# Softmax of seven units: exponential head by head out of the scores' bank

## The chip, the cores and the metric

One core of one Trainium2 chip. The metric is the device time of one execution in microseconds; the kernel before takes 1047.18 us as the median of three runs (1046.12 to 1047.91).

## The reference

Attention over pooled keys and values, then two gated feed-forward blocks. Cut to what matters:

```
k_p, v_p = k, v averaged over groups of 8 positions        # 72 pooled positions per head
scores   = (q @ k_p^T) / 8                                 # 4 batches, 8 heads, 576 queries
scores   = scores - max(scores, axis=-1)
attn     = exp(scores);  attn /= sum(attn, axis=-1) + 1e-9
x        = attn @ v_p, heads side by side                  # 2304 tokens x 512
x        = (silu(xn @ w_gate) * (xn @ w_val)) @ w_out      # xn: x normalised, d_ff = 1536
out      = ((x @ w_a) * (x @ w_b)) @ w_out2
```

## The kernel before

The 2304 tokens are cut in two ways. Attention works in nine units of 256 tokens (u = 0 to 8), each of two halves of 128 tokens (i = 0, 1). The first feed-forward block works on five tiles of 512, 256, 512, 512 and 512 tokens; per tile it goes through twelve hidden blocks f of 128: a gate product g, a value product v (12 matmuls each, every operand split in a high and a low part, hence wh and wl, xh and xl), a Silu of g on ScalarE, its product with v on VectorE (ht), the split of that product (hh on ScalarE, hl on VectorE), and the output product (acc, 12 matmuls). A bank each belongs to g, v and the four parts of acc; two banks (tag `att`) are shared by everything that attention puts into PSUM: transposed queries (qT), scores (sc), transposed exponentials (eT), the result (xT) and small sums.

Softmax of a unit, in `score_steps`: the queries are transposed and copied to SBUF (`q_transpose`), then `scores` makes two banks for each half, sc_0 and sc_1, with four heads of 72 columns in each. VectorE takes the maximum of each head (L328) and writes scores minus maximum into the SBUF tile e (L329). For units 2 to 8 `exponent` then runs one Exp over e of both halves (L335, 128 x 1152, in place), and `normalise` sums e per head (L340), adds 1e-9 (L341), takes reciprocals (L342) and multiplies (L343). Units 0 and 1 do this half by half. `value_steps` transposes e (eT) and multiplies it by the pooled values.

Attention of later units runs beside the feed-forward tiles. In tile 0 the order in which steps are emitted is a written list of tokens (FIRST), in tile 1 a second list, afterwards merged lists. The scheduler of the framework then sets each engine's queue: it places instructions by readiness and priority, so what stands in a queue can differ from the order in the source. Every engine works its own queue strictly in that order. Weights arrive as 64-bit words that ScalarE, VectorE and GpSimd turn into fp32 together (L590, L591 on ScalarE; L597, L600 on VectorE; L607 on GpSimd), and are split by ScalarE (L621) and GpSimd or VectorE (L622). The second feed-forward block (lines from L1015 on) starts at about 615 us and has no attention beside it.

ScalarE's functions live in tables; an ACT_TABLE_LOAD stands in its queue wherever the next function is not in the loaded one. Exp and Silu never share one here, while copies, casts, Square and Abs run under either.

Of the kernel before, what the change touches and what calls it, by code (L numbers as in the profile page):

```python
# [8 lines left out]
F32 = mybir.dt.float32  # L9
# [4 lines left out]
AF = mybir.ActivationFunctionType  # L14
ALU = mybir.AluOpType
AX = mybir.AxisListType

P = 128
# [4 lines left out]
FINE = 2  # L23
# [41 lines left out]
def attention_moe_moe2(  # L65
# [14 lines left out]
    nc = tc.nc  # L80
    B, H, S, D = q.shape
# [11 lines left out]
    QK_SCALE = 1.0 / float(D) ** 0.5  # L93
# [15 lines left out]
    sm_p = attn.enter_context(tc.tile_pool(name="sm", bufs=1, side="right"))  # L109
# [3 lines left out]
    for t0, n in starts(TILES1):  # L113
# [9 lines left out]
        out=mask, in_=mask, pattern=[[P, NV], [-SP, H]], compare_op=ALU.is_ge,  # L123
# [3 lines left out]
        out=mask, in_=mask, pattern=[[-P, NV], [SP, H]], compare_op=ALU.is_ge,  # L127
# [15 lines left out]
    def att_bank(name, tag=None):  # L143
        if tag is not None:
            pass
        else:
            tag = boot["banks"].pop(0) if boot["banks"] else "att"
        return ps.tile([P, 512], F32, tag=tag, name=name, bufs=2 if tag == "att" else 1)
# [118 lines left out]
    def runs(t0, n):  # L267
        done = 0
        while done < n:
            b, s = divmod(t0 + done, S)  # L270
            step = min(n - done, S - s)
            yield done, step, b, s
            done += step

    NU = NT // UNIT
    NS = UNIT // P
    q_t, e_t, xf_t = {}, {}, {}

    def load_q(sub):
        if sub >= NT // P:  # L280
            return
        t = at_p.tile([P, H, D], F32, tag="q", name=f"q_{sub}")
        for off, cnt, b, s in runs(sub * P, P):
            nc.sync.dma_start(
                out=t[off:off + cnt], in_=q[b, :, s:s + cnt, :].rearrange("h p d -> p h d")
            )
        q_t[sub] = t

    def score_steps(u):
        box = {}  # L290

        def q_transpose(i):
            sub = u * NS + i
            if i == 0:
                e_t[u] = at_p.tile([P, NS, H, SP], F32, tag="e", name=f"e_{u}")
            bank = att_bank(f"qT_{sub}")
            qs = q_t.pop(sub)
            for p in range(NP):
                nc.tensor.transpose(
                    bank[:, p * P:(p + 1) * P],  # L300
                    qs[:, 2 * p:2 * p + 2, :].rearrange("p a d -> p (a d)"),
                    ident,
                )
            if boot["on"] and i % 2:
                qT = h_p.tile([P, NP, P], F32, tag="ht", name=f"qTs_{sub}", bufs=1)
            else:
                qT = at_p.tile([P, NP, P], F32, tag="qT", name=f"qTs_{sub}", bufs=1)
            nc.scalar.copy(qT.rearrange("p a t -> p (a t)"), bank)
            box["qT"] = qT
            box["m"] = sm_p.tile([P, H, 1], F32, tag="m", name=f"m_{sub}", bufs=2)  # L310
            load_q(sub + NS)

        def scores(i, hf):
            sub, e, m, qT = u * NS + i, e_t[u], box["m"], box["qT"]
            sc = att_bank(f"sc_{sub}_{hf}")
            for off, cnt, b, s in runs(sub * P, P):
                for a in range(2):
                    p = 2 * hf + a
                    nc.tensor.matmul(  # L319
                        sc[off:off + cnt, a * 2 * SP:(a + 1) * 2 * SP],  # L320
                        qT[:, p, off:off + cnt],
                        KB[b % 2][:, p, :],
                        start=True,
                        stop=True,
                    )
            scv = sc[:, :4 * SP].rearrange("p (h s) -> p h s", h=4)
            mh = m[:, 4 * hf:4 * hf + 4, :]
            nc.vector.reduce_max(out=mh.rearrange("p h o -> p (h o)"), in_=scv, axis=AX.X)  # L328
            nc.vector.tensor_sub(  # L329
                e[:, i, 4 * hf:4 * hf + 4, :], scv, mh.to_broadcast([P, 4, SP])  # L330
            )

        def exponent(lo, hi):
            e = e_t[u][:, lo:hi].rearrange("p i h s -> p (i h s)")
            nc.scalar.activation(out=e, in_=e, func=AF.Exp, scale=QK_SCALE)  # L335

        def normalise(lo, hi):
            ev = e_t[u][:, lo:hi].rearrange("p i h s -> p (i h) s")
            sums = sm_p.tile([P, NS * H, 1], F32, tag="sums", name=f"sum_{u}")[:, :(hi - lo) * H]
            nc.vector.reduce_sum(out=sums.rearrange("p h o -> p (h o)"), in_=ev, axis=AX.X)  # L340
            nc.vector.tensor_scalar_add(sums, sums, 1e-9)  # L341
            nc.vector.reciprocal(sums, sums)  # L342
            (nc.gpsimd if boot["alt"] else nc.vector).tensor_mul(  # L343
                ev, ev, sums.to_broadcast([P, (hi - lo) * H, SP])
            )

        steps = []
        for i in range(NS):
            steps += [lambda i=i: q_transpose(i)]
            if u < FINE:  # L350
                steps += [lambda i=i, h=h: scores(i, h) for h in range(2)]
                steps += [lambda i=i: exponent(i, i + 1), lambda i=i: normalise(i, i + 1)]
            else:
                steps += [lambda i=i: (scores(i, 0), scores(i, 1))]
        if u >= FINE:
            steps += [lambda: exponent(0, NS), lambda: normalise(0, NS)]
        return steps

    def value_steps(u, dest):
# [312 lines left out]
    def dest(u):  # L672
        t = u * UNIT
        for idx, (t0, n) in enumerate(starts(TILES1)):
            if t0 <= t < t0 + n:
# [4 lines left out]
                return get  # L680

    A = [score_steps(u) for u in range(NU)]
    V = [value_steps(u, dest(u)) for u in range(NU)]
    loads, prep = zip(*(prep_steps(b) for b in range(B)))
# [497 lines left out]
    for idx, (ph, t0, n) in enumerate(work):  # L1182
# [26 lines left out]
        for f, cols, last, ahead, own in jobs:  # L1209
            m = cols.stop - cols.start  # L1210
# [31 lines left out]
        for c, acc in enumerate(accs):  # L1242
            ev = ev_p.tile([P, 512], F32, tag="ev", name="ev")
# [45 lines left out]
```

## Time and profile before

| | |
|---|---|
| median of three runs | 1047.18 us |
| the profiled execution, its own time | 1046.91 us |
| its span | 1045.0 us |
| mean granted TensorE clock | 0.98 of full speed |
| busy: TensorE, weight loads | 978.8 us (94%), 858.4 us (82%) |
| busy: VectorE, ScalarE, GpSimd | 663.0 us (63%), 477.0 us (46%), 453.0 us (43%) |

The profiled execution's own time is its span and 1.9 us around it. The shares are means over stages with different limits: the first 300 us have attention, weight conversion and the first tile beside each other, the stretch from 300 to 600 us is nearly all feed-forward matmuls. PE is TensorE, PEld its weight loads, DVE VectorE, ACT ScalarE, POOL GpSimd.

### The profile page before, as it was taken

Reading aid. Unit: us, or ns where it says so; the run is one execution under the profiler, and the core shown is the slowest. Engines: PE = TensorE matmul, PEld = TensorE weight load, DVE = VectorE, ACT = ScalarE, POOL = GpSimd, SP = SyncE. Lnnn points to the kernel's source line nnn. Section 1 sums busy time; section 2 is a strip of 40 time slices with the busy share of each in tenths; the row PEclk is TensorE's granted clock in tenths of the full one; section 3 lists DMA queues with packets and bytes.
Section 4 is the critical chain, followed back from the end, with each engine's and each line's share of the span. In section 5 each row is a group of like instructions: output and inputs, shape, how many; then the busy total and the mean of one; then the engine's idle time right before and its main releaser. Section 6 shows DMA issues by size and latency. Waiting matters only on the chain.

```text
span 1045.0 us, 13959 instructions
## 1 busy us (share of the span) xinstructions
PE 978.8 (94%) x5044; PEld 858.4 (82%) x5044; DVE 663.0 (63%) x992; ACT 477.0 (46%) x900; POOL 453.0 (43%) x360
## 2 busy tenths in 40 slices
PE   4977899889899999999999988999999998999998
PEld 3766677778788887888788878999999998888886
DVE  6999988996853756363627859766677665322221
ACT  3765764565454536444445435443444434222211
POOL 6476584646543434343359834533334332310000
PEclk9799899999899999999999999999999999999999
DMA  9456534330100002000111133434444444544332
GB/s 231 138 178 192 168 105 123 108 90 2 31 10 21 1 1 61 1 1 1 41 43 60 41 109 99 142 124 152 126 145 143 131 126 170 182 139 136 126 117 74
DMA packets 82804, 101.57 MB, mean 97 GB/s; under 512 B 24112, under 2 KB 63024, under 8 KB 82736
## 3 DMA queue, kind: packets, MB, share of 16 engines
q1 hardware_dynamic: 82736, 100.69, 31.3%
q8 instruction: 40, 0.66, 0.3%
q14 instruction: 28, 0.23, 0.1%
HBM read 73.93 MB, written 26.74 MB: 96 GB/s over the span
## 4 chain that ended last, share of the span: by engine, by line
PE 72%; DVE 18%; issue 3%; DMA 3%; ACT 2%; POOL 1%; SPq 1%; DVEq 0%; ACTq 0%; POOLq 0%
PE o L1114 14%; PE X L1015 13%; PE acc L663 9%; PE g L650 9%; PE v L650 9%; PE Y L1015 6%; PE Z L1015 3%; PE xT L400 2%; PE g L788 2%; DVE wf L600 2%; DVE kp L190 1%; PE sc L319 1%; PE v L788 1%; DVE wf L597 1%; DVE x L874 1%
## 5 line engine op out<-in xcount | busy, mean ns | idle before, releaser
L622 POOL TENSOR_TENSOR wl<-wf,wh 128x512 fp32r<-128x512 f32 x163 | 225.5, 1391 | 226.2 <-ACT wh L621 223.7
L621 ACT CAST wh<-wf 128x512 fp32r<-128x512 f32 x180 | 109.3, 619 | 72.6 <-PE acc L663 32.4
L663 PE MATMUL acc<-hh,wl 128*128 128x512 f32 (+1 forms) x248 | 92.2, 372 | 8.9 <-ACT hh L1231 5.7
L1094 DVE TENSOR_TENSOR hl<-hf,hh 128x768 fp32r<-128x768 f32 x36 | 35.6, 993 | 96.5 <-ACT hh L1093 96.5
L663 PE MATMUL acc<-hl,wh 128*128 128x512 f32 (+1 forms) x248 | 90.2, 368 | 3.6 <-DVE hl L806 3.4
L663 PE MATMUL acc<-hh,wh 128*128 128x512 f32 (+1 forms) x248 | 90.4, 365 | 0.0
L1114 PE MATMUL o<-woh,hl 128*128 128x512 f32 x216 | 86.0, 398 | 0.0
L1114 PE MATMUL o<-woh,hh 128*128 128x512 f32 x216 | 85.3, 395 | 0.0
L1114 PE MATMUL o<-wol,hh 128*128 128x512 f32 x216 | 84.9, 393 | 0.0
L650 PE MATMUL v<-xh,wl 128*128 128x512 f32 (+1 forms) x192 | 72.6, 378 | 2.8 <-DVE ht L1228 2.7
L1093 ACT CAST hh<-hf 128x768 fp32r<-128x768 f32 x36 | 29.8, 834 | 93.6 <-PE o L1114 87.0
L650 PE MATMUL g<-xh,wl 128*128 128x512 f32 (+1 forms) x192 | 71.4, 372 | 0.0
L650 PE MATMUL g<-xl,wh 128*128 128x512 f32 (+1 forms) x192 | 70.8, 369 | 0.1
L650 PE MATMUL g<-xh,wh 128*128 128x512 f32 (+1 forms) x192 | 70.9, 369 | 0.0
L650 PE MATMUL v<-xl,wh 128*128 128x512 f32 (+1 forms) x192 | 69.9, 364 | 0.0
L650 PE MATMUL v<-xh,wh 128*128 128x512 f32 (+1 forms) x192 | 69.6, 363 | 0.0
L607 POOL TENSOR_TENSOR wf<-wf,st 128x512 int32<-128x512 int32 x36 | 52.8, 1467 | 37.2 <-DVE wf L600 17.8
L607 POOL TENSOR_TENSOR w<-w,st 128x512 int32<-128x512 int32 x24 | 31.9, 1331 | 78.5 <-DVE w L600 77.3
L663 PEld LDWEIGHTS acc<-hh,wl 128*128 128x128 f32 x248 | 47.4, 191 | 17.5 <-issue 6.9
L1023 ACT COPY p<-X 128x384 f32<-128x384 f32 x36 | 17.2, 478 | 89.3 <-PE X L1015 89.3
L663 PEld LDWEIGHTS acc<-hl,wh 128*128 128x128 f32 x248 | 46.8, 191 | 12.8 <-DVE hl L806 4.5
L1228 DVE TENSOR_TENSOR ht<-ht,v 128x512 f32<-128x512 f32 (+1 forms) x48 | 29.6, 616 | 42.1 <-PE v L650 40.9
(208 smaller groups left out, 2782.7 us busy)
## 6 DMA issues: line engine op xcount, KB each, us to landing
hf<-h SPq DMA_DIRECT2D x36, 384.0 KB
st<-in_moe_w_out_dram SPq DMA_DIRECT2D x24, 512.0 KB
h<-u SPq DMA_DIRECT2D x36, 192.0 KB
h<-p SPq DMA_DIRECT2D x36, 192.0 KB
st<-in_moe_w_gate_dram SPq DMA_DIRECT2D x12, 512.0 KB
st<-in_moe_w_val_dram SPq DMA_DIRECT2D x12, 512.0 KB
st<-in_moe_w_a_dram SPq DMA_DIRECT2D x12, 512.0 KB
st<-in_moe_w_b_dram SPq DMA_DIRECT2D x12, 512.0 KB
```

The source lines that it names most:

```text
L400: nc.tensor.matmul(bank[:, off:off + cnt], lhs, rhs, start=(i == 0), stop=(i == len(pairs) - 1),)
L607: nc.gpsimd.tensor_tensor(out=bits, in0=bits, in1=low, op=ALU.add)
L621: nc.scalar.copy(wh, wf[ph, f, i])
L622: (nc.vector if boot["alt"] else nc.gpsimd).tensor_sub(wl, wf[ph, f, i], wh.bitcast(F32))
L650: nc.tensor.matmul(bank[:, :n], w[:, c, :], x[:, c, cols], start=(i == 0), stop=(i == 3 * KD - 1),)
L663: nc.tensor.matmul(accs[c][:, cols], w[:, c, :], x[:, :n], start=(f == 0 and i == 0 and cols.start == 0), stop=(f == NF - 1 and i == 2),)
L788: nc.tensor.matmul(bank[:, :n], w[:, c, :], x[:, c, cols], start=(c == 0 and i == 0), stop=(c == KD - 1 and i == 2),)
L1015: nc.tensor.matmul(dst[:, :HALF], w[:, c0 + c, :], x[:, c, :], start=(start and i == 0), stop=(stop and i == 5), skip_group_check=True,)
L1093: nc.scalar.copy(hh, hf)
L1094: nc.vector.tensor_sub(hl, hf, hh.bitcast(F32))
L1114: nc.tensor.matmul(accs[i], x[:, sub], y, start=(f == 0 and j == 0), stop=(f == NF - 1 and j == 2),)
L1228: nc.vector.tensor_mul(ht[:, :m], ht[:, :m], vb[:, :m])
```

## The change

For units 2 to 8 the subtraction, the one Exp over e and the separate sum go away. VectorE still takes the maximum of four heads, then multiplies the 128 x 4 maxima by minus the scale; ScalarE runs one Exp per head (128 x 72) straight from the scores' bank, with the negative maximum as a per-partition bias, and its accumulator output gives that head's sum. The step in which the Exp stood is now empty; `normalise` starts at the addition of 1e-9. The lists of tokens are the same.

```diff
--- before.py
+++ after.py
@@ -326,6 +326,17 @@
             scv = sc[:, :4 * SP].rearrange("p (h s) -> p h s", h=4)
             mh = m[:, 4 * hf:4 * hf + 4, :]
             nc.vector.reduce_max(out=mh.rearrange("p h o -> p (h o)"), in_=scv, axis=AX.X)
+            if u >= FINE:
+                if i == 0 and hf == 0:
+                    box["sums"] = sm_p.tile([P, NS * H, 1], F32, tag="sums", name=f"sum_{u}")
+                nc.vector.tensor_scalar_mul(mh, mh, -QK_SCALE)
+                for h in range(4):
+                    j = 4 * hf + h
+                    nc.scalar.activation(
+                        out=e[:, i, j, :], in_=scv[:, h, :], func=AF.Exp, scale=QK_SCALE,
+                        bias=m[:, j], accum_out=box["sums"][:, i * H + j],
+                    )
+                return
             nc.vector.tensor_sub(
                 e[:, i, 4 * hf:4 * hf + 4, :], scv, mh.to_broadcast([P, 4, SP])
             )
@@ -336,8 +347,11 @@
 
         def normalise(lo, hi):
             ev = e_t[u][:, lo:hi].rearrange("p i h s -> p (i h) s")
-            sums = sm_p.tile([P, NS * H, 1], F32, tag="sums", name=f"sum_{u}")[:, :(hi - lo) * H]
-            nc.vector.reduce_sum(out=sums.rearrange("p h o -> p (h o)"), in_=ev, axis=AX.X)
+            if u >= FINE:
+                sums = box["sums"]
+            else:
+                sums = sm_p.tile([P, NS * H, 1], F32, tag="sums", name=f"sum_{u}")[:, :(hi - lo) * H]
+                nc.vector.reduce_sum(out=sums.rearrange("p h o -> p (h o)"), in_=ev, axis=AX.X)
             nc.vector.tensor_scalar_add(sums, sums, 1e-9)
             nc.vector.reciprocal(sums, sums)
             (nc.gpsimd if boot["alt"] else nc.vector).tensor_mul(
@@ -353,7 +367,7 @@
             else:
                 steps += [lambda i=i: (scores(i, 0), scores(i, 1))]
         if u >= FINE:
-            steps += [lambda: exponent(0, NS), lambda: normalise(0, NS)]
+            steps += [lambda: None, lambda: normalise(0, NS)]
         return steps
 
     def value_steps(u, dest):
```

The queues are set anew by the scheduler. In the built program ACT has 28 table loads where there were 16: one pair for unit 2 as before, and for each of units 3 to 8 a load for Exp and one for Silu around each half's eight Exps. The next two places are in unit 2, which runs beside tile 0.

On PE, where the gate product of one hidden block (g, weights of block 6) and the output product of an earlier one (acc, weights of block 4) meet; before:

```order
L788 MATMUL g<-xh,wl_1104 128x512
L788 MATMUL g<-xh,wh_1103 128x512
L788 MATMUL g<-xl,wh_1103 128x512
L663 MATMUL acc_543<-hh,wl_1100 128x512
L663 MATMUL acc_543<-hh,wh_1099 128x512
L663 MATMUL acc_543<-hl,wh_1099 128x512
L663 MATMUL acc_544<-hh,wl_1100 128x512
```

and in the changed kernel:

```order
L677 MATMUL acc_546<-hh,wl_1117 128x512
L677 MATMUL acc_546<-hh,wh_1116 128x512
L677 MATMUL acc_546<-hl,wh_1116 128x512
L382 MATMUL eT_0_1255<-ident,e_588 128x128
L802 MATMUL g<-xh,wl_1121 128x512
L802 MATMUL g<-xh,wh_1120 128x512
L802 MATMUL g<-xl,wh_1120 128x512
```

The gate product stood ahead of the output product and now stands behind it, and a transpose of e (eT_0) has come between the two. The scores of half 1 moved too: they stood between the first four and the last eight matmuls of the output product one pass earlier, and now stand after the sixth matmul of the value product that follows it, with six matmuls of that product and the twelve of the output product behind them.

On POOL, from the conversion of block 7's gate weights to that of block 8's output weights (wl is the low part of a split, wf a conversion); before:

```order
L607 TENSOR_TENSOR wf_0_7_1051<-wf_0_7_1051,st_7_0_905 128x512
L607 TENSOR_TENSOR wf_0_7_1061<-wf_0_7_1061,st_7_1_973 128x512
L622 TENSOR_TENSOR wl_1100<-wf_0_4_838,wh_1099 128x512
L607 TENSOR_TENSOR wf_0_7_1079<-wf_0_7_1079,st_7_2_1026 128x512
L607 TENSOR_TENSOR wf_0_8_1123<-wf_0_8_1123,st_8_0_1049 128x512
L607 TENSOR_TENSOR wf_0_8_1138<-wf_0_8_1138,st_8_1_1059 128x512
L607 TENSOR_TENSOR wf_0_8_1193<-wf_0_8_1193,st_8_2_1077 128x512
```

and now:

```order
L621 TENSOR_TENSOR wf_0_7_1060<-wf_0_7_1060,st_7_0_905 128x512
L621 TENSOR_TENSOR wf_0_7_1070<-wf_0_7_1070,st_7_1_973 128x512
L621 TENSOR_TENSOR wf_0_7_1088<-wf_0_7_1088,st_7_2_1035 128x512
L636 TENSOR_TENSOR wl_1117<-wf_0_4_838,wh_1116 128x512
L621 TENSOR_TENSOR wf_0_8_1140<-wf_0_8_1140,st_8_0_1058 128x512
L621 TENSOR_TENSOR wf_0_8_1155<-wf_0_8_1155,st_8_1_1068 128x512
L621 TENSOR_TENSOR wf_0_8_1209<-wf_0_8_1209,st_8_2_1086 128x512
```

The split of block 4's output weights has gone behind the conversion of block 7's output weights (st_7_2). That conversion waits for its step L600 on DVE, which in both kernels stands behind the maximum of sc_0 of half 1.

On DVE, the end of unit 4's softmax beside tile 1 (ss collects squares of unit 3's result, el_4 and hl are low parts); before:

```order
L1228 TENSOR_TENSOR ht<-ht,v 128x256
L381 TENSOR_TENSOR el_4_2277<-eT_4_2273,eh_4_2276 64x256
L411 TENSOR_TENSOR ss_2073<-ss_2073,sq_2_2288 128x256
L1232 TENSOR_TENSOR hl<-ht,hh 128x256
L340 TENSOR_REDUCE sum_2333<-e_1789 128x16
L411 TENSOR_TENSOR ss_2073<-ss_2073,sq_3_2313 128x256
L341 TENSOR_SCALAR sum_2333<-sum_2333 128x16
L342 RECIPROCAL sum_2333<-sum_2333 128x16
L343 TENSOR_TENSOR e_1789<-e_1789,sum_2333 128x1152
L1228 TENSOR_TENSOR ht<-ht,v 128x256
```

and now:

```order
L1242 TENSOR_TENSOR ht<-ht,v 128x256
L395 TENSOR_TENSOR el_4_2321<-eT_4_2317,eh_4_2320 64x256
L425 TENSOR_TENSOR ss_2101<-ss_2101,sq_2_2332 128x256
L1246 TENSOR_TENSOR hl<-ht,hh 128x256
L355 TENSOR_SCALAR sum_2167<-sum_2167 128x16
L356 RECIPROCAL sum_2167<-sum_2167 128x16
L357 TENSOR_TENSOR e_1817<-e_1817,sum_2167 128x1152
L425 TENSOR_TENSOR ss_2101<-ss_2101,sq_3_2357 128x256
L1242 TENSOR_TENSOR ht<-ht,v 128x256
```

The sum is gone, and the addition, the reciprocal and the normalising product have come ahead of the last sum of squares. The maxima of half 1 have moved the other way: behind three reductions of kv_2 and kv_1 (L190) that they stood ahead of.

In units 5 to 8 what next needs a scores' bank has moved back on PE: in unit 5 the queries' transpose stood six matmuls of 512 columns behind the scores of half 0 and now stands fifteen behind.

## Rows read from the trace of the kernel before

**Rows 1.** Stretches: start and end, length, each engine's busy time (instructions), TensorE's granted clock, DMA share

```profile
100.00:130.00 30.00, 25.15 (x111) 19.82 (x110) 28.60 (x43) 23.46 (x38) 16.53 (x11) 0.89 0.55 166
...
170.00:245.00 75.00, 62.79 (x438) 57.25 (x437) 69.64 (x98) 42.70 (x81) 40.90 (x29) 0.98 0.28 81
...
280.00:460.00 180.00, 177.77 (x889) 147.55 (x888) 98.91 (x165) 87.35 (x157) 70.76 (x53) 1.00 0.06 16
```

**Rows 2.** Waits of PE: line, releaser, total us, times, longest us

```profile
PE eT L368 <- DVE e L343: 4.1, 3, 2.3
...
PE g L788 <- DVE wl L622: 3.3, 1, 3.3
...
PE xT L400 <- ACT sq L410: 1.2, 1, 1.2
```

**Rows 3.** ACT groups by shape: busy us, mean ns, idle before

```profile
L335 ACT ACT_TABLE_LOAD x7 | 9.0, 1283 | 0.1
...
L335 ACT ACTIVATE e<-e 128x1152 f32<-128x1152 f32 x7 | 8.2, 1168 | 3.0 <-DVE e L329 2.8
...
L335 ACT ACTIVATE e<-e 128x576 f32<-128x576 f32 x4 | 2.8, 693 | 3.1 <-DVE e L329 3.1
```

**Rows 4.** Timeline of ACT, two reads of one bank: start us, duration us

```profile
232.56 0.47 ACT L404 ACTIVATE xf<-xT,gneg 128x256 f32<-128x256 f32 x1
232.93 0.37 ACT L410 ACTIVATE sq<-xT 128x256 f32<-128x256 f32 x1
```

**Rows 5.** Timeline of ACT, a table load and the Exp behind it

```profile
290.75 1.28 ACT L335 ACT_TABLE_LOAD   x1
292.05 1.17 ACT L335 ACTIVATE e<-e 128x1152 f32<-128x1152 f32 x1
```

**Rows 6.** DVE groups by shape: busy us, mean ns, idle before

```profile
L328 DVE TENSOR_REDUCE m<-sc 128x4 f32<-128x288 f32 x36 | 16.0, 451 | 20.4 <-PE sc L319 20.2
L329 DVE TENSOR_TENSOR e<-sc,m 128x288 f32<-128x288 f32 x36 | 15.3, 448 | 0.1
...
L343 DVE TENSOR_TENSOR e<-e,sum 128x1152 f32<-128x1152 f32 x7 | 12.9, 1839 | 0.1
...
L190 DVE TENSOR_REDUCE vp<-kv 128x64 f32<-128x512 f32 x10 | 10.4, 1073 | 0.0
...
L340 DVE TENSOR_REDUCE sum<-e 128x16 f32<-128x1152 f32 x7 | 9.4, 1345 | 0.1
...
L341 DVE TENSOR_SCALAR sum<-sum 128x16 f32<-128x16 f32 x7 | 4.4, 636 | 0.0
```

**Rows 7.** Timeline of DVE and POOL, a small addition beside GpSimd's work

```profile
413.60 1.27 DVE L341 TENSOR_SCALAR sum<-sum 128x16 f32<-128x16 f32 x1
...
413.07 3.02 POOL L622 TENSOR_TENSOR wl<-wf,wh 128x512 fp32r<-128x512 f32 x2 [3.26 <-ACT wh L621]
```

**Rows 8.** Timeline of PE, DVE and POOL in unit 2: start us, duration us

```profile
117.45 0.76 PE L788 MATMUL g<-xh,wl 128*128 128x512 f32 x1 [3.31 <-DVE wl L622]
...
122.70 0.54 PE L663 MATMUL acc<-hh,wl 128*128 128x512 f32 x1
...
125.59 0.39 PE L788 MATMUL v<-xh,wl 128*128 128x512 f32 x1
125.82 0.39 PE L788 MATMUL v<-xh,wh 128*128 128x512 f32 x1
...
112.49 1.43 DVE L600 SCALAR_TENSOR_TENSOR wf<-st,wf 128x512 int32<-128x512 int32 x1
...
113.33 1.73 POOL L622 TENSOR_TENSOR wl<-wf,wh 128x512 fp32r<-128x512 f32 x1
115.03 1.72 POOL L607 TENSOR_TENSOR wf<-wf,st 128x512 int32<-128x512 int32 x1
```

## The prediction

> **What bounds the kernel now.** I read the stretches first, to find where units 2 to 8 meet a busy engine [rows 1]. Three stages differ. From 100 to 130 us (unit 2) DVE works 28.60 of 30 us and PE 25.15. From 170 to 245 us (units 3 and 4) DVE works 69.64 of 75 us, PE 62.79, ACT 42.70: DVE sets the pace. From 280 to 460 us (units 5 to 8) PE works 177.77 of 180 us, DVE 98.91, ACT 87.35: there at most 2.2 us can be gained, and the question is what delays PE. The waits of PE name what it lacked [rows 2]: 3.3 us for a weight split that DVE made (unit 2), 4.1 us in three waits for the normalised e, the longest 2.3 us, 1.2 us for ACT's square. Then the groups by shape give prices [rows 3, 6], and the timelines give distances [rows 4, 5, 7, 8]. The reader is to see that the same microsecond on ACT or DVE is worth something before 245 us and nothing after 280 us, unless PE stands behind it.
>
> **The price of one small Exp.** The trace has no Exp of 72 columns, none out of PSUM with a bias and none with an accumulator, so I bound it. The Exp costs 1168 ns at 1152 columns and 693 at 576 [rows 3]: 0.825 ns per column. A read of a bank with a per-partition operand takes 0.47 us at 256 columns, and the next one starts 0.37 us after it [rows 4]; 184 columns fewer are 0.15 us less, so 0.22 us from start to start is the low end. If the sum is read out by an instruction as long as the whole plain read (0.37 us) it is 0.59, the high end. I take 0.38: the low end and what is fixed in the plain read (0.37 less 256 x 0.825 ns, 0.16 us). Eight are then 3.0 us (1.8 to 4.7), all 112 are 43 us.
>
> **ACT as a whole.** Added 43 us and twelve table loads of 1.283 us (28 for 16), 15.4 us; removed seven Exps of 1.168 us, 8.2 us [rows 3]. That is 50 us more on an engine that was busy for 477 of 1045: it stays no bound as a whole, and only places count. A load ends 0.02 us before the Exp behind it starts (290.75 + 1.28 against 292.05) [rows 5], so 1.28 us is all that I see of one. The Trainium skill, "ScalarE: Activation LUTs", section "What ACT_TABLE_LOAD costs", puts a switch of sets at 2.66 us with a drain, and its rule is to group calls by set, which speaks against this change. By it the twelve would be 31.9 us instead of 15.4; the rows show no such drain, and I go by the rows.
>
> **DVE as a whole.** Removed 28 subtractions of 0.448 us, 12.5 us, and seven sums of 1.345 us, 9.4 us [rows 6]. Added 28 multiplications of 128 x 4. Their nearest row is the addition on 128 x 16: 636 ns in the mean, but 1.27 us where GpSimd was splitting weights beside it [rows 6, 7]; without that company the seven leave 0.16 us for one (three of 1.27 and four of 0.16 give the mean). So the added part is 4.5 to 35.6 us, 17.8 at the mean; the net is -17.4 to +13.7, and I take -4.1. The Trainium skill, "SBUF — State Buffer", section "Who interferes with whom", says that a tensor_scalar in its two-port mode and GpSimd block each other outright, and that a reduction never does. The row agrees; by the rule the change swaps sums that cannot be blocked for small instructions that can.
>
> **Unit 2, beside tile 0.** PE ran out of work at 114.14 us (117.45 less 3.31) and then did the gate product, at half clock from 117.45 to 122.70, 5.25 us, and the output product by 125.59, 2.89 us at full clock [rows 8]. In the new queue the output product comes first, so that wait could be filled. But its split on POOL now stands behind a conversion that waits for L600 on DVE, which waits for the maximum of half 1's scores. These scores end six matmuls (1.4 us at the pitch of 0.23 us) [rows 8] before the point where PE would run out: 112.7 us at the earliest. Then maximum 0.45, L600 1.43, conversion 1.72, split 1.73 [rows 6, 8]: 118.1 us. With the half-clock pass and the other at full clock PE is done at 126.2 us against 125.59. The transpose eT_0 between the two needs the whole softmax; from 112.7 us two maxima, L600, two multiplications, two weight splits on DVE of at most 1.7 us each, four Exps, addition and product (1.84) take some 10 us, which the output product (until 123.3) covers. Cost +0.7 us. If L600 takes 0.4 us less it is 0.3; if each Exp takes 0.59 us, ACT is 1.7 us later with the copy of half 1's queries, which stands behind the eight Exps of half 0, and it is +2.4. I take +1.
>
> **Units 3 and 4, beside tiles 0 and 1.** DVE loses eight subtractions and two sums, 6.3 us, and gets eight multiplications, 1.3 to 10.2 us, 5.1 at the mean [rows 6]: net -5.0 to +3.9, taken as -1.2. In unit 4 the maxima of half 1 get three reductions of 1.07 us ahead [rows 6], and the Exps behind them take 3.0 us for 1.17. Against that the product with the reciprocals no longer waits for a sum (1.345) and a sum of squares, and 2.3 us of waiting for it are there to be saved [rows 2]. These two nearly cancel; I take -1.5 us for both units, between -5 and +4. What was late next there is the reductions of k and v, which wait for their loads in either kernel.
>
> **Units 5 to 8, beside tiles 2 and 3.** Two banks serve all of attention, and a scores' bank is now free only when its four Exps have read it. Needed from the scores' end: two maxima 0.90, two multiplications 0.32, four Exps 1.5, together 2.7 us. There: fifteen matmuls of 0.23, 3.5 us. So 0.8 us to spare; at 0.59 us an Exp it is 3.6 us, 0.1 late, and each multiplication that meets a split on POOL adds 1.1. Silu comes later by the eight Exps and two loads (5.6 us for 3.7), but the gate bank that it frees is wanted only after a value and an output product of twelve matmuls each, 5.5 us. I take +0.5 us over all eight halves; the ends are -2 and +10.
>
> **Sum.** +1 -1.5 +0.5 = 0 on the profiled execution's 1046.9 us, which lies 0.3 us under the median of 1047.18. Forecast 1047.0 us: no change that can be told. A measurement of this kernel can tell about 0.2%, 2.1 us.
>
> **Rivals.** First, faster: the relief of DVE counts in full. For it: DVE's 93% share from 170 to 245 us, and three of the long waits of PE are behind DVE. Against it: the reductions there wait for loads, and the multiplications can be blocked. If none is blocked: -5.0 in units 3 and 4 and nothing lost in unit 2, 1042 us.
>
> Second, slower: the scores' banks hold PE. The place is the transpose behind each half's scores from unit 5 on; it decides from about 0.48 us an Exp, with one multiplication in two blocked (0.636 each instead of 0.16). Then the need is 0.90 + 1.27 + 2.36 = 4.5 us against 3.5, 1.0 us at each of eight halves, 8 us; with +2.4 in unit 2 and -1.5 in units 3 and 4 it is 1055.8 us. For it: PE has no slack there, and what it loses stays lost. Against it: ACT is free half of the time in that stretch [rows 1].
>
> Third, slower in unit 2 alone: the split behind L600 comes later than I have it, since ACT converts weights behind the eight Exps too. A DVE or POOL instruction more ahead of it (1.43, 1.72) gives 1049 to 1050 us, with the rest as forecast.
>
> **How the numbers follow.** Forecast 0.45, faster rival 0.25, banks 0.20, unit 2 alone 0.10. Of the forecast's 0.45, some 0.36 lies within 0.2%, 0.05 below and 0.04 above. So faster 0.30, same 0.36, slower 0.34. The range takes in the faster rival's time and most of the way to the banks' time: 1041.5 to 1055.0; the forecast's own range is 1044 to 1050.
>
> **What would show it.** A small Exp near 0.38 us from start to start, 112 of them, and 28 table loads; small multiplications of 0.16 us with some at 1.27; in unit 2 the wait on PE at acc instead of g, for POOL; the 2.3 us wait of eT for e in unit 4 gone or under 1 us; in units 5 to 8 no wait of PE for an Exp over 0.5 us. I am wrong if PE waits for L335 in that stretch by more than 3 us in all, if an Exp takes over 0.5 us, or if PE's busy time from 170 to 245 us shows a gain of 4 us and more.

## The result, and the profile after

The changed kernel takes 1054.47 us (median of 6 runs, 1053.25 to 1057.06) against 1047.55 us of the kernel before beside it (6 runs): a ratio of 1.0074, 95% interval 1.0054 to 1.0094. It is 7 us slower where I had forecast no change. The profiled execution took 1057.06 us, span 1055.3 us; it is the slowest of the six, so I read places from it and sizes from the medians.

The same three stretches as in [rows 1], in the changed kernel (start and end, length, busy time of PE, PEld, DVE, ACT and POOL with instructions, granted clock, DMA share):

```profile
100.00:130.00 30.00, 23.83 (x109) 18.11 (x108) 25.72 (x39) 24.93 (x66) 14.70 (x11) 0.94 0.51 153
170.00:245.00 75.00, 62.35 (x399) 56.58 (x398) 60.34 (x98) 50.87 (x138) 34.75 (x25) 0.92 0.29 82
280.00:460.00 180.00, 176.27 (x873) 146.03 (x874) 91.60 (x156) 109.70 (x277) 74.17 (x53) 0.98 0.07 18
```

From 170 to 245 us DVE is busy 9.3 us less than before, more relief than I had forecast, and PE has done no more work for it. PE stands idle there for nearly as long as before (12.65 of 75 us, 12.21 before), but its clock went from 0.98 to 0.92: 0.06 of 75 us is 4.5 us. What PE lacked there (waits from 170 to 245 us: line, releaser, total us, times, longest):

```profile
PE v L802 <- POOL wl L636: 4.2, 1, 4.2
PE xT L414 <- DVE el L395: 3.0, 1, 3.0
PE v L664 <- DVE ht L1242: 1.2, 1, 1.2
PE g L664 <- ACT ht L1234: 1.0, 2, 0.8
PE eT L382 <- ACT e L335: 0.9, 1, 0.9
PE xT L414 <- ACT e L335: 0.8, 1, 0.8
PE acc L677 <- DVE hl L1246: 0.7, 1, 0.7
...
PE qT L299 <- ACT e L335: 0.3, 1, 0.3
```

The wait of eT for the normalised e, 2.3 us in [rows 2], is gone, as intended. In its place stand a new wait of 4.2 us for a weight split (unit 3) and short waits for the exponential itself at eT, xT and qT (unit 4).

The groups of ACT and DVE that answer to [rows 3, 6] (busy us, mean ns, idle before and its releaser):

```profile
L335 ACT ACTIVATE e<-sc,m 128x72 f32<-128x72 f32 x112 | 34.1, 329 | 2.5 <-DVE m L332 2.3
...
L335 ACT ACTIVATION_READ_ACCUMULATOR e<-sc,m 128x1 f32 x112 | 24.1, 215 | 0.0
...
L335 ACT ACT_TABLE_LOAD x13 | 16.7, 1283 | 20.6 <-DVE m L332 20.5
```

```profile
L332 DVE TENSOR_SCALAR m<-m 128x4 f32<-128x4 f32 x28 | 10.6, 394 | 0.1
```

Before, the load had no idle time ahead of it (0.1 us) and the Exp behind it waited (3.0 us) [rows 3]: the load ran while DVE was still subtracting. Now the load itself waits for the maximum, 20.5 us in all, and its 1.28 us start only then. The new Exp waits for two engines (DVE for the maximum, PE for the bank). The wait for the maximum is an instruction of its own in this program (28 of 17 ns in ACT's queue at L335, EVENT_SEMAPHORE in the trace), and where a load is needed it stands ahead of the load.

**Unit 3.** ACT and POOL in the changed kernel; start us, duration us, idle time and releaser in brackets:

```profile
173.57 1.28 ACT L335 ACT_TABLE_LOAD   x1 [4.83 <-DVE m L332]
174.87 0.32 ACT L335 ACTIVATE e<-sc,m 128x72 f32<-128x72 f32 x1
175.09 0.19 ACT L335 ACTIVATION_READ_ACCUMULATOR e<-sc,m 128x1 f32 x1
175.18 0.31 ACT L335 ACTIVATE e<-sc,m 128x72 f32<-128x72 f32 x1
...
177.25 2.21 ACT L635 CAST wh<-wf 128x512 fp32r<-128x512 f32 x4
...
177.98 6.69 POOL L636 TENSOR_TENSOR wl<-wf,wh 128x512 fp32r<-128x512 f32 x4 [8.70 <-PE g L802]
```

and PE at the end of it, with the stretch behind its wait:

```profile
178.23 0.60 PE L299 MATMUL qT<-ident,q 128*128 128x128 f32 x4
182.98 0.80 PE L802 MATMUL v<-xh,wl 128*128 128x512 f32 x1 [4.15 <-POOL wl L636]
183.58 0.63 PE L802 MATMUL v<-xh,wh 128*128 128x512 f32 x1
...
188.76 0.39 PE L802 MATMUL v<-xh,wh 128*128 128x512 f32 x1
188.99 0.39 PE L802 MATMUL v<-xl,wh 128*128 128x512 f32 x1
```

```profile
183.00:188.00 5.00, 5.00 (x15) 4.39 (x16) 2.40 (x5) 1.40 (x2) 1.67 (x1) 0.50 0.26 93
```

and the same five microseconds before:

```profile
183.00:188.00 5.00, 4.11 (x20) 3.09 (x18) 5.00 (x5) 2.82 (x6) 1.67 (x2) 1.00 0.32 108
```

Four weight casts stand behind the eight Exps in ACT's queue. They start 3.7 us after the maximum (load and eight Exps), POOL splits them one after the other, and PE waits 4.15 us. After the wait its matmuls are spaced 0.42 us (183.58 to 184.00) instead of 0.23 (188.76 to 188.99): the stretch from 183 to 188 us has a granted clock of 0.50, the lower of the two levels (1.2 GHz), where before had 1.00.

**Unit 4.** PE, then ACT:

```profile
228.95 0.66 PE L299 MATMUL qT<-ident,q 128*128 128x128 f32 x4 [0.28 <-ACT e L335]
...
239.42 0.41 PE L382 MATMUL eT<-ident,e 128*64 128x128 f32 x2 [0.90 <-ACT e L335]
240.63 0.39 PE L414 MATMUL xT<-el,vh 128*128 128x256 f32 x1 [0.80 <-ACT e L335]
```

```profile
236.75 1.28 ACT L335 ACT_TABLE_LOAD   x1 [1.01 <-DVE m L332]
238.05 0.32 ACT L335 ACTIVATE e<-sc,m 128x72 f32<-128x72 f32 x1
...
238.95 0.32 ACT L335 ACTIVATE e<-sc,m 128x72 f32<-128x72 f32 x1
...
240.13 0.35 ACT L335 ACTIVATE e<-sc,m 128x72 f32<-128x72 f32 x1
240.59 1.28 ACT L1234 ACT_TABLE_LOAD   x1
```

eT and xT start as soon as the fourth and the eighth Exp have read their banks (239.3 and 240.5 us): the two attention banks were taken. From 234 to 244 us PE works only 6.74 of 10 us, and then the clock falls. The changed kernel:

```profile
234.00:244.00 10.00, 6.74 (x45) 5.88 (x45) 7.60 (x14) 8.65 (x28) 4.15 (x4) 0.93 0.10 24
244.00:254.00 10.00, 10.00 (x64) 9.55 (x63) 6.92 (x12) 5.70 (x13) 8.84 (x7) 0.72 0.01 2
```

and the kernel before:

```profile
234.00:244.00 10.00, 6.83 (x47) 6.38 (x48) 9.17 (x14) 5.70 (x13) 7.82 (x6) 0.92 0.01 3
244.00:254.00 10.00, 10.00 (x80) 9.90 (x80) 5.46 (x19) 4.94 (x13) 4.71 (x4) 0.91 0.00 0
```

PE was idle there as long before (3.17 of 10 us, now 3.26), with a wait of 2.3 us for the normalised e. So PE's idle time hasn't grown, it lies at other places, and the clock behind it is lower: in the second rows PE is fully busy at a mean of 0.72 where it had 0.91, 1.9 us. Nor do all of the waits stand behind the banks: of the 3.7 us from 220 to 260 us, the three behind L335 are 2.0; g waits 1.0 us for a Silu, one of its two times (0.8 us) for the one that stands behind the eight Exps and a load, and acc 0.7 us for hl on DVE.

### The profile page after: what moved, and what is told of

Its sections match the earlier page's. It is cut to its first block, busy times and chain, and to the rows that moved or that the text cites. A ratio compares the mean times of both kernels' runs of the same rounds, so it can differ in the third digit from the quotient of the medians.

```text
span 1055.3 us, 14205 instructions
## 1 busy us (share of the span) xinstructions
PE 985.8 (93%) x5044; PEld 863.4 (82%) x5044; DVE 650.4 (62%) x985; ACT 516.9 (49%) x1129; POOL 456.7 (43%) x360
## 4 chain that ended last, share of the span: by engine, by line
PE 72%; DVE 15%; issue 4%; ACT 4%; DMA 2%; POOL 2%; SPq 1%; ACTq 0%; DVEq 0%; POOLq 0%
PE o L1128 14%; PE X L1029 13%; PE g L664 9%; PE acc L677 9%; PE v L664 9%; PE Y L1029 6%; PE Z L1029 3%; PE xT L414 3%; DVE wf L614 2%; PE sc L319 1%; DVE wf L611 1%; POOL wl L636 1%; PE v L802 1%; PE g L802 1%; DVE x L888 1%
## 5 line engine op out<-in xcount | busy, mean ns | idle before, releaser
L636 POOL TENSOR_TENSOR wl<-wf,wh 128x512 fp32r<-128x512 f32 x163 | 229.5, 1419 | 229.4 <-ACT wh L635 205.3
```

What stands on the lines that cost most here:

```text
L636: (nc.vector if boot["alt"] else nc.gpsimd).tensor_sub(wl, wf[ph, f, i], wh.bitcast(F32))
```

## The experiments

Theory A: the place in ACT's queue (weight casts behind the Exps). Theory B: the price of 112 Exps. C: place times price. D: the scores' banks, held by ACT until the last Exp. E: the bank as input (late load, slower reading). Each ratio is to the kernel before, timed beside it (medians 1046.47 to 1047.55 us). "Lag" is how much later the same matmul starts than in the profile before; units_5_to_8 is the kernel before up to 280 us and still drifts by 2.4 us, so a smaller change of lag in one profile tells nothing.

**place_cheap**: only the place.

```diff
  e[:, i, 4 * hf:4 * hf + 4, :], scv, mh.to_broadcast([P, 4, SP])
  )
+ if u >= FINE:
+     eh = e[:, i, 4 * hf:4 * hf + 4, :].rearrange("p h s -> p (h s)")
+     nc.scalar.activation(out=eh, in_=eh, func=AF.Exp, scale=QK_SCALE)
...
- steps += [lambda: exponent(0, NS), lambda: normalise(0, NS)]
+ steps += [lambda: None, lambda: normalise(0, NS)]
```

> Keeps the subtraction and the sum on VectorE; only the exponential is moved, one of 288 columns per half in every unit from 2 on, right behind the half's subtraction. It stands in ScalarE's queue where the changed kernel has its eight small ones, in unit 3 ahead of the same four weight casts. Theory A (the place in the queue: ScalarE waits for the scores with the weight casts behind it): TensorE still waits for the low half of the value weights of block 11 in unit 3, 2 to 4 us (4.15 in the changed kernel, less some 1.5 us that the cheaper exponentials give back), and the kernel is 3 to 6 us over the kernel before. Theory B (the price: 112 exponentials at 0.5 us with their sums): the price is gone, so the wait is gone and the time is within 1 us of before.

Measured 1042.7 us, ratio 0.9957 (0.9940 to 0.9975): faster than before. Theory A alone has fallen. Its ACT in unit 3 shows why the place was harmless:

```profile
165.58 1.28 ACT L334 ACT_TABLE_LOAD   x1
170.63 0.81 ACT L334 ACTIVATE e<-e 128x288 f32<-128x288 f32 x2 [3.77 <-DVE e L329]
171.35 1.65 ACT L624 CAST wh<-wf 128x512 fp32r<-128x512 f32 x3
```

ACT waits about as long, but with the load done, and the casts follow 0.7 us after its wait ends instead of 3.7.

**price_old_place**: only the price.

```diff
  def exponent(lo, hi):
+     if u >= FINE:
+         for i in range(lo, hi):
+             for j in range(H):
+                 nc.scalar.activation(
+                     out=e_t[u][:, i, j, :], in_=e_t[u][:, i, j, :], func=AF.Exp,
+                     scale=QK_SCALE, accum_out=box["sums"][:, i * H + j],
+                 )
+         return
```

> Keeps the subtraction on VectorE and the exponential's old place behind both token blocks of a unit, but splits it into 16 per unit of 72 columns, each with its sum accumulated (no sum on VectorE): the price of the changed kernel at the old place. Theory A (place): ScalarE doesn't wait with casts behind it, so no wait for the weights in units 2 and 3; only the unit's own chain is some 4 to 7 us longer (16 at about 0.3 us or 0.5 us instead of 1.2 us), which the slack of units 5 to 8 takes; 0 to +3 us against before. Theory B (price): the loss comes back, +5 us or more.

Measured 1045.93 us, 0.9986 (0.9975 to 0.9997). The price alone costs nothing either (251 ns an Exp here, from SBUF and without a bias, for 329 in the changed kernel); theory B has fallen.

**late_unit3**: `late()` issues a block's stored Exps at the head of the next step, in unit 3 alone.

> The changed kernel, but in unit 3 the eight exponentials of a token block are issued one step later, behind the weight casts that the order lists between (the banks are held that long). Same number and price. Theory A (place): the 4.15 us wait for the low half of the value weights in unit 3 goes or falls below 1 us, and the kernel is 2 to 4 us faster than the changed one (some 1050.5 to 1052.5 on its median of 1054.5). Theory B (price): the time stays within 1 us of the changed kernel.

Measured 1054.13 us, 1.0065 (1.0047 to 1.0083). The 4.15 us wait was gone, the time was not: half a miss. In its profile unit 4 lost 4.1 us of lag instead.

**units_5_to_8**: `if u >= 5` in place of `if u >= FINE`.

> The change in units 5 to 8 only; units 2, 3 and 4 as before. By the lag of the same matmuls between the two traces the stretch of units 5 to 8 lost some 1.4 us: Theory A (place, in units 2 to 4 where casts of weights that are due stand behind) 0 to +2 us against before. Theory B (price per exponential): four of the seven units carry four sevenths of the loss, +4 us.

Measured 1048.64 us, 1.0013 (1.0000 to 1.0026): some 1.4 us of the seven lie in units 5 to 8.

**place_and_price**: place, number and sums of the changed kernel and nearly its price (an Exp every 0.25 us for 0.30); the bank is read by DVE.

```diff
- nc.vector.tensor_scalar_mul(mh, mh, -QK_SCALE)
+ nc.vector.tensor_sub(
+     e[:, i, 4 * hf:4 * hf + 4, :], scv, mh.to_broadcast([P, 4, SP])
+ )
...
-         out=e[:, i, j, :], in_=scv[:, h, :], func=AF.Exp, scale=QK_SCALE,
-         bias=m[:, j], accum_out=box["sums"][:, i * H + j],
+         out=e[:, i, j, :], in_=e[:, i, j, :], func=AF.Exp, scale=QK_SCALE,
+         accum_out=box["sums"][:, i * H + j],
```

> The changed kernel, except that the subtraction of the maximum stays on VectorE (no small multiplication) and the eight exponentials of a block read its result, not the bank. So place, number, price and accumulated sums are those of the changed kernel, and ScalarE's order in unit 3 is the same; but the banks are given back by VectorE, and the exponential waits for one engine only, so that its table load stands ahead of the wait. Theory C (ScalarE is held with casts and Silus behind it: place times price): most of the loss stays, +3 to +6 us against the kernel before (some 1050.5 to 1053.5). Theory D (the banks are held until the last exponential, or the table load runs only after the maximum): the loss goes, -3 to +1 us.

Measured 1045.1 us, 0.9979 (0.9967 to 0.9991). Theory C has fallen: what costs is that ACT reads the bank (D or E). Nine microseconds lie between this kernel and the changed one.

**one_shift**: one maximum for four heads, one Exp of 288 columns per bank, read from the bank.

> One maximum over the four heads of a half, and one exponential of 288 columns per half straight from the bank with it as bias; the sums stay on VectorE. (A softmax doesn't depend on the shift, so the same quotients are computed.) No subtraction, bank held by ScalarE as in the changed kernel, table load behind the maximum as there, but a fourth of the exponentials and no accumulated sums. Theory C: the price goes, and with it most of the loss; -3 to +2 us. Theory D: banks and late load stay; +3 us or more.

Measured 1046.88 us, 1.0002 (0.9993 to 1.0011). Under D as I had put it (banks and late load stay) it should have lost 3 us or more. It does less work than place_cheap (no subtraction) and is 4 us slower, but not slower than before: with one wide Exp the bank is held, yet for a shorter time (table below). So D can stand only if the length of the hold counts. The run also speaks against the late load alone: its loads wait for the maximum too, 16.1 us in all, and in unit 3 as long as the changed kernel's (4.82 us, then load and Exps):

```profile
L332 ACT ACT_TABLE_LOAD x14 | 18.0, 1283 | 16.2 <-DVE m L331 16.1
```

**early_load**: one Exp of 2 columns on `sc[:, :2]` ahead of the maximum.

> The changed kernel with one more exponential of 2 columns per block, on the first half's bank: it waits for TensorE alone, and so the table load ahead of it waits for nothing and runs while the scores are still due. Everything else as in the changed kernel. If the load behind the maximum is what turns the changed kernel's place into a loss (11 of its 13 loads at 1.28 us end a wait for the maximum), 2 to 5 us come back against 1054.5. If it is the eight exponentials and their sums (some 2.4 us a block), less than 1.5 us does.

Measured 1056.98 us, 1.0098 (1.0081 to 1.0115). Nothing came back, though no load waits any more (0.3 us ahead of all fourteen for Exp). The banks of unit 4 are hardly free any sooner (table below), and the second maximum of a block now waits for ACT, which it didn't in the changed kernel, so the run doesn't settle by itself what the late load costs.

**place_from_3**: place_cheap with `u > FINE`.

> As the kernel with one exponential of 288 columns per half behind its subtraction (1042.7 us), but from unit 3 on; unit 2 as before. There TensorE waited 3.0 us in unit 2 for the low half of the out weights, as in the changed kernel (3.5 us). If that wait is lost time, this is 1 to 3 us faster again, 1040 to 1041.7; if it only stands in place of another, the same as 1042.7.

Measured 1043.55 us, 0.9966 (0.9952 to 0.9981), no different from place_cheap: unit 2's wait only stands in place of another.

**hold_bank**: place_and_price with a late reader.

```diff
+ hold = sm_p.tile([P, 2], F32, tag="hold", name=f"hold_{sub}_{hf}")
+ nc.scalar.activation(
+     out=hold, in_=sc[:, :2], func=AF.Exp, scale=0.0,
+     bias=box["sums"][:, i * H + j],
+ )
```

> The kernel place_and_price (subtraction on VectorE, eight exponentials with sums from its result; 1045.1 us), with one thing more: behind each half's last exponential ScalarE reads 2 columns of the half's bank once, made to wait for the last sum. So the bank is held as long as in the changed kernel; the exponential's input, its table load ahead of the wait and ScalarE's order in unit 3 are those of place_and_price. Theory D (banks held until the last exponential): the loss comes back, 1050 to 1056 us. Theory E (it is the bank as input: the table load behind the maximum, and the slower reading): 1045 to 1047 us, only 28 more small instructions.

Measured 1056.19 us, 1.0093 (1.0079 to 1.0106). Theory D, against E: the input, the load and the order are those of the fast kernel, and two columns read late bring 11 us. (Four more table loads, 34 for 30, are a part of that.)

**copy_first**: `tensor_copy` of the scores after the multiplication; the Exps read the copy.

> The changed kernel, but VectorE copies each half's scores out of the bank, and the eight exponentials, with the negative maximum as bias and the sums, read the copy. VectorE does more than before the change in each half (maximum, multiplication, copy), ScalarE the same as in the changed kernel; the bank is given back by the copy. Theory D: the loss goes although nothing was saved, 1044 to 1048 us. If the small multiplication or the longer ScalarE work is the cause: 1050 us or more. Theory E would have it gone too, since the load stands ahead of the wait here.

Measured 1052.69 us, 1.0049 (1.0031 to 1.0068): a miss for D, which had it free of loss. Its lag grew by 6.1 us in unit 4 and hardly elsewhere. There the copy, behind DVE's other work, came so late that the second pair of banks was still held for 5.7 us (table below); that this is the reason is argued, no run shows it. Its Exps also took longer (one every 0.34 us, from SBUF with a bias), which is no part of D and isn't ruled out as a share.

**no_accumulation**: without `accum_out`, sums on DVE as before.

> The changed kernel without the accumulated sums: VectorE sums as before. The exponentials start some 0.1 us closer (no reading of the accumulator), so a bank is held some 0.4 us less, and VectorE gets its 12.5 us back. Theory D: most of the loss stays, +4 to +7 us against the kernel before, since the bank's hold is mostly the load, the wait and the exponentials themselves. If the accumulation is the cause: 0 to +2 us.

Measured 1056.38 us, 1.0090 (1.0074 to 1.0105): the accumulated sums are not the cause, without them it is rather worse.

**hold_unit_4**: hold_bank with `if u != 4: return` ahead of the late reading.

> place_and_price (1045.1 us), with the late reading of the bank by ScalarE in unit 4 alone. The stretch 225 to 260 us of that kernel gained 1.25 us on the kernel before, that of hold_bank lost 7.1. If the held bank costs most where tile 1 runs, between PE's many short waits there: 4 to 8 us come, 1049 to 1053. If the loss of hold_bank was the sum over all units: 1 to 2 us, 1046 to 1047.

Measured 1054.51 us, 1.0079 (1.0057 to 1.0101), 9 us over place_and_price from one unit of seven. Here the late reading of each block's second bank fell behind a Silu and brought a table load, two in all, and PE's longest waits from 222 to 262 us are 3.8 us for el on DVE and 2.1 us for a Silu. So the run overstates the changed kernel's share, and its loss isn't the held bank's alone.

**changed_but_unit_4**: the changed kernel with place_and_price's lines `if u == 4`.

> The changed kernel, with unit 4 alone as in place_and_price (VectorE subtracts and so gives the bank back, the exponentials with their sums read the result). If unit 4's held bank is the main cost: 3 to 5 us come back, 1049.5 to 1051.5. If the cost is spread over the units: 1 us, 1053.5.

Measured 1050.51 us, 1.0038 (1.0025 to 1.0050): 4 of the 7 us come back. Unit 4's two stretches in this kernel, and PE's waits from 220 to 260 us:

```profile
234.00:244.00 10.00, 8.75 (x66) 7.94 (x67) 9.78 (x15) 8.87 (x31) 6.47 (x5) 1.00 0.05 14
244.00:254.00 10.00, 9.41 (x82) 9.21 (x81) 8.22 (x22) 5.34 (x15) 6.29 (x5) 1.00 0.01 2
```

```profile
PE eT L393 <- DVE e L333: 1.1, 1, 1.1
PE g L675 <- ACT ht L1245: 0.6, 1, 0.6
PE eT L393 <- DVE el L406: 0.6, 1, 0.6
PE eT L393 <- DVE e L368: 0.3, 1, 0.3
```

PE waits 2.6 us in all (3.7 in the changed kernel, by the rows for g, eT, xT, acc L1246 and qT; 3.5 before), and its clock stays at 1.00 where the changed kernel had 0.93 and 0.72. The stretch from 226 to 260 us of before, and where the same work lies in the changed kernel and in this one:

```profile
226.00:260.00 34.00, 30.45 (x234) 29.28 (x233) 24.35 (x49) 19.89 (x42) 16.91 (x13) 0.95 0.13 40
230.40:267.30 36.90, 33.44 (x243) 31.60 (x242) 23.92 (x48) 24.55 (x64) 19.95 (x15) 0.91 0.12 37
228.60:261.40 32.80, 30.11 (x242) 28.60 (x242) 24.74 (x49) 23.01 (x62) 19.68 (x15) 1.00 0.15 45
```

PE is idle for 3.55, 3.46 and 2.69 us. Of the 4.1 us between the last two, 3.3 are matmuls that took longer at the lower clock and 0.8 is idle time. The profiled execution of this kernel is the fastest of its twelve, so these sizes are those of one execution each; the 4 us is by the medians. The edit takes the late load and the bias column out of unit 4 together with the long hold.

**changed_but_3_and_4**: the same `if u in (3, 4)`.

> As changed_but_unit_4, with unit 3 so too. Left of the change as it is: unit 2 (1.4 us by the lag of the same matmuls) and units 5 to 8 (1.1 us, where the time alone gave +1.1). So 1047 to 1050; if it stays above 1052, the held bank of units 3 and 4 isn't what the change loses by.

Measured 1048.54 us, 1.0013 (0.9999 to 1.0026): another 2 us. The wait for the weight split in unit 3 fell with it from 4.2 to 2.0 us; there the load stands ahead of the wait again, and the Exps are shorter:

```profile
PE v L813 <- POOL wl L647: 2.0, 1, 2.0
```

**mix**: unit 2 as before, units 3 and 4 as place_cheap, units 5 to 8 as place_and_price.

> A version put together from what was fast in each stretch: unit 2 as before, units 3 and 4 with one exponential of 288 columns per half behind its subtraction, units 5 to 8 with subtraction on VectorE and eight exponentials with accumulated sums per block. By the lags of the same matmuls, place_from_3 stands 6.9 us ahead of before at the end of the first stage, and place_and_price gains 2.7 us in units 5 to 8 where that one gains 1.4: 1041 to 1043.5 us.

Measured 1041.08 us, 0.9944 (0.9924 to 0.9963): 6 us faster than before and 13 than the changed kernel. Its lead over place_cheap is within the intervals.

The bank's hold in unit 4, worked out from each trace: from the start of a block's first scores matmul to the end of the last reading of its two banks, for the unit's two blocks. Beside it the change of the lag over that stretch (226 to 260 us of before).

| kernel | hold, us | lag, us |
|---|---|---|
| before | 3.1, 4.8 | 0 |
| place_cheap | 2.4, 3.6 | +0.8 |
| place_and_price | 2.4, 4.2 | -1.3 |
| changed_but_unit_4 | 2.4, 4.0 | -1.3 |
| one_shift | 4.0, 5.2 | +0.4 |
| copy_first | 3.0, 5.7 | +6.1 |
| no_accumulation | 5.4, 6.8 | +2.3 |
| changed | 6.2, 8.0 | +2.8 |
| late_unit3 | 6.2, 8.2 | +4.1 |
| early_load | 5.9, 7.2 | +3.3 |
| hold_bank | 8.0, 7.8 | +7.1 |
| hold_unit_4 | 8.0, 7.8 | +8.5 |

The kernels not listed held the banks for at most 4.5 us and lie between -1.9 and +1.6. Up to 5.2 us nothing is lost that one profile could tell; from 5.7 us on each kernel loses, 2.3 to 8.5 us, the smallest of these near the drift. The size of the loss doesn't follow the hold (6.1 us at 5.7, 2.8 at 8.0), a hold also grows when PE itself is slow, and it is unit 4 alone: in units 5 to 8 the changed kernel holds its banks for 5.5 to 7.2 us and loses 1.4 us in all.

## Why the prediction was wrong

**The step that failed** is "units 3 and 4, -1.5 us". With both lifted out of the change 6 us come back (1.0074 to 1.0013), and in the profile the lag grows by 5.6 us from 170 to 260 us of before, so it was about +6. The step priced DVE's relief and ACT's extra time. It left out that the Exps take the two banks away from the transposes beside them; I had priced that for units 5 to 8 alone, because PE is full there. And it had no term for the clock. The wait of 2.3 us that was to be saved in unit 4 did go, but waits for the Exps and for what stands behind them on ACT and DVE came in its place, PE's idle time stayed what it was, and the clock behind it was lower. That the Exps out of the bank in these units cost the time is shown by the runs that lift them out; that the length of the hold does it rests on hold_bank and hold_unit_4, which carry further table loads, and on the table. Why the clock fell lower after as much idle time stays open.

Unit 3's share (2 us) comes with the four casts behind the load and eight Exps, 3.7 us after the maximum. That the load is behind the maximum stands in the trace. It isn't the cause by itself: one_shift has it too, with casts 2.1 us after the maximum, and is no slower than before. How the share divides between load, Exps and banks no run shows.

**The rival "the banks hold PE"** had a part of the mechanism and, by luck, the size (1055.8 us against 1054.47), at the wrong place. The need of 2.7 us in the forecast and the rival's 4.5 both left out the load: 1.28 us that I had seen run during a wait [rows 3, 5] and took to stay there. The rival's condition was also worked out wrongly: with 0.90 for the maxima and 1.27 for the multiplications, four Exps fill the 3.5 us from 0.33 us each on, not from 0.48. In the places it named, PE waited for L335 0.9 + 0.4 us in all, under the 3 us that I had set, and the loss was 1.4 us.

**The price of a small Exp** was too high: 0.30 us from start to start (174.87 to 175.18 and on), not 0.38, the reading of the sum included. ACT's busy time rose by 39.9 us, not 50.

**The small multiplications** took 0.394 us in the mean (median 0.169, longest 1.25), 11 us for 17.8. All nine that took over 0.5 us ran beside a weight split on POOL, as the prediction had it, and three of these are in unit 4, ahead of its Exps. DVE's relief was so larger than forecast, and PE did no more work for it: "DVE sets the pace", which the prediction and its faster rival read from the 93% share, failed on that.

**Unit 2** went as forecast: PE's wait moved to acc for POOL's split (3.55 us, until 119.00 against 118.1), and v started at 127.42 against 126.2; the lag over the unit is 1.4 us, for +1. place_from_3 shows that the wait alone isn't lost time.

**Units 5 to 8**: +0.5 forecast, +1.4 measured, inside my ends. The grouping rule of the Trainium skill ("ScalarE: Activation LUTs", "Table sets: the hidden batching unit"), which I had set aside as to size, didn't decide the time. The kernel place_cheap has 30 loads where before has 16, and is 4.5 us faster. All loads show 1283 ns.

Not settled: about 1.7 us by which the profiled changed kernel fell further back after 605 us, in work that wasn't changed.

## What to carry to other kernels

Before a reader of a shared bank is moved to another engine, work out how long the bank then stays taken, from the first write to the last read, with every wait and table load between, and do it for each place where the banks are wanted, the stretches with gaps in PE first. A short wait of PE is not priced by its length: look at the granted clock behind it, and at the same work in the kernel before, which may have waited there as long. And when an instruction comes to wait for a second engine, ask what stood hidden in front of its first wait.

## What the runs showed of the hardware

- An Exp with an accumulated sum is two rows, the second one ACTIVATION_READ_ACCUMULATOR (215 ns in the mean); the two overlap with the next Exp, so busy times add up to 0.52 us where the pitch is 0.30.
- An Exp of 72 columns with a bias column takes 329 ns from a bank (pitch 0.30 us) and 342 from SBUF (copy_first, first row below, pitch 0.34); from SBUF without a bias it takes 250 (place_and_price, the other rows, pitch 0.25). So the bank is not the slower source; the longer rows go with the bias.

```profile
L336 ACT ACTIVATE e<-e,m 128x72 f32<-128x72 f32 x112 | 38.2, 342 | 9.7 <-DVE m L332 8.0 <-DVE e L333 1.4
L337 ACT ACTIVATE e<-e 128x72 f32<-128x72 f32 x112 | 27.9, 250 | 8.0 <-DVE e L332 7.9
L337 ACT ACTIVATION_READ_ACCUMULATOR e<-e 128x1 f32 x112 | 21.0, 188 | 0.0
```

- In these programs a table load runs ahead of the wait where the Exp behind it waits for one engine (0.2 us of idle time ahead of place_cheap's twelve, 0.1 before), and behind the first wait where it waits for two (20.5 us here, 16.1 in one_shift).
- After an idle time of 4.15 us PE ran at half clock for 5 us (0.50). After several short waits, 3.26 of 10 us, it ran at 0.72 over the next 10; in the kernel before, after 3.17 of 10 us in other places, at 0.91.
